# A retention layer with routed adapters: from 128-token steps to 64-token steps with state and v stacked over the partitions, in a fixed order

## The chip, the cores and the metric

The kernel runs on one core of a Trainium2 chip. The metric is the device time of one execution in microseconds (us), and of several executions the median. Engines are named as in the profile: PE is TensorE's matmul and PEld its weight load, DVE is VectorE, ACT is ScalarE, POOL is GpSimd, SP is SyncE, whose queue issues nearly all transfers.

## What is computed

Eight batches of eight heads, 576 tokens, 64 values per head. A causal linear attention with a decay per head, then, for each of the 4608 tokens, a low-rank adapter step over its 512 values: eight adapters of rank 16, of which the two with the highest gate value are used.

```python
scores = q @ k.T / 8                     # per batch and head, 576 x 576
ret = scores * gamma[h] ** (i - j)       # for j <= i, else 0
x = ret @ v                              # heads side by side: 4608 x 512
logits = x @ w_gate                      # 4608 x 8, the best two kept
w = softmax of those two
out = x + sum over the two e of  w[e] * (x @ A[e]) @ B[e]
```

## The kernel before

All arithmetic is f32 but for the last two small products of the adapters, which are fp16. Tokens are cut in chunks of 128: four full chunks and one of 64. A unit is one chunk of two batches (16 heads), so there are 16 units of 128 tokens and then 4 units of 64 tokens, 20 in all, ordered by chunk. Inputs are loaded by quads, two units at a time (L127; the last chunk at L148), with three buffers for each of q, k and v. Each f32 product of two matrices is one call and shows as two records in the profile; a transpose is one.

What is done for a unit:

- scale_v (L197, POOL): v is multiplied by gamma to the power of minus the token's place in the chunk.
- stage_T (L229): PE turns q and k, 16 calls each, into tiles with the head's values on the partitions; DVE takes q out of PSUM and multiplies it by gamma to the power of the token's place (L241), ACT copies k (L250).
- stage_S (L291): the scores, 16 calls with 64 rows of contraction (the values of one head), 128 output rows and 128 columns; DVE masks them, four operations of 128x512 (L302).
- stage_O: where there is a state, its product with q goes into px, 16 calls of 64 rows, 64 output rows, 128 columns (L359). Then the update of the state, k's transpose times v, 16 calls of 128 rows, 64 output rows, 64 columns (L373). DVE adds it to the old state (L387), and POOL decays the sum (L388).
- stage_R (L408): scores times v, on top of px, 16 calls of 128 rows, 64 output rows and 128 columns; ACT copies px to xT (L417).
- stage_Z (L447): x times the adapters' A and the gate, 8 calls of 128x128 with 136 columns; DVE finds the best two and forms the weighted result zc (L460 to L479), with ACT's sigmoid between (L468).
- stage_X (L493, L498): zc turned and copied. stage_B (L512): x turned back to one token per row, 16 calls. stage_Y (L533): the adapters' B added on top; ACT copies the result out (L543), and SP stores it (L548).

In a unit of 64 tokens, the two batches lie in the two halves of the partitions. Its scores are 64x64 tiles with 64 columns (L291 again, 16 calls, row half by head parity and column half by batch, the head parity changing at every call), and so are its state product (L341) and its R (L426).

The order of the main loop is written out as the lines below show, but the instructions are placed by a scheduler that may let stages of neighbouring units mix, and PSUM tiles come from one pool of eight banks:

```python
stage_S(t); scale_v(t + 1); stage_O(t); stage_R(t)
stage_T(t + 1); stage_B(t - 1); stage_X(t - 1)
stage_Z(t); stage_Y(t - 1)
```

The whole kernel before, with the profile's line numbers:

Of the kernel before, what the change touches and what calls it, by code (L numbers as in the profile page):

```python
# [13 lines left out]
AFT = mybir.ActivationFunctionType  # L15


@with_exitstack
def kernel(
# [17 lines left out]
    NP = B // 2  # L37
    NFULL = S // 128
    LH = S - 128 * NFULL
    QUAD = 4  # L40
    NQ = B // QUAD

    scale = 1.0 / float(np.sqrt(Dh))
    gam = 1.0 - 2.0 ** (-5.0 - np.arange(H, dtype=np.float64))
    jj = np.arange(128, dtype=np.float64)

    ident32_np = np.eye(128, dtype=np.float32)
    tri_np = (jj[None, :] >= jj[:, None]).astype(np.float32)
    j64 = np.arange(128) % 64
    i64 = np.arange(64)  # L50
    trih_np = (i64[None, :] >= j64[:, None]).astype(np.float32)
    aqp_np = np.zeros((128, HP, 128), dtype=np.float32)
    g128_np = np.zeros((128, HP), dtype=np.float32)
    for hp in range(HP):
        for ho in range(2):
            g = gam[2 * hp + ho]
            aqp_np[64 * ho : 64 * ho + 64, hp, :] = scale * g ** jj[None, :]
            g128_np[64 * ho : 64 * ho + 64, hp] = g**128.0
    gv_np = np.stack([gam[h] ** (-jj) for h in range(H)], axis=1).astype(np.float32)
    gvh_np = np.stack([gam[h] ** (-j64.astype(np.float64)) for h in range(H)], axis=1).astype(  # L60
        np.float32
    )
    i64_np = np.concatenate([np.eye(64), np.eye(64)], axis=0).astype(np.float32)
    first_np = i64_np
    rest_np = np.concatenate(
        [ident32_np, tri_np, trih_np, gv_np, gvh_np, g128_np], axis=1
    ).astype(np.float32)
    NPK = rest_np.shape[1]
    dr_first = nc.inline_tensor(first_np, "c_first")
    dr_rest = nc.inline_tensor(rest_np, "c_rest")  # L70
    dr_aqp = nc.inline_tensor(aqp_np, "c_aqp")
# [4 lines left out]
    mo = ctx.enter_context(tc.tile_pool(name="moe", bufs=3))  # L76
    pp = ctx.enter_context(tc.tile_pool(name="pp", bufs=8, space=bass.MemoryType.PSUM))

    id64 = cpool.tile([128, 64], FP32, tag="id64", name="id64")
    nc.sync.dma_start(out=id64, in_=dr_first.ap())  # L80
    warm = cpool.tile([128, 1], FP32, tag="warm", name="warm")
    nc.vector.memset(warm, 0.0)
    nc.scalar.activation(out=warm, in_=warm, func=AFT.Sigmoid)
    pack = cpool.tile([128, NPK], FP32, tag="pack", name="pack")
    aqp = cpool.tile([128, HP, 128], FP32, tag="aqp", name="aqp")
    ident32 = pack[:, 0:128]
    tri = pack[:, 128:256]
    trih = pack[:, 256:320]
    gv = pack[:, 320 : 320 + H]
    gvh = pack[:, 320 + H : 320 + 2 * H]  # L90
    g128 = pack[:, 320 + 2 * H : 320 + 2 * H + HP]

    AW = []
    for par in range(2):
        AW.append(cpool.tile([128, HP, ER + E], FP32, tag=f"AW{par}", name=f"AW{par}"))
    Bcat = cpool.tile([128, Dm], FP16, tag="Bcat", name="Bcat")
    ident16 = cpool.tile([128, 128], FP16, tag="ident16", name="ident16")

    def load_moe():
        for dt in range(HP):  # L100
            nc.sync.dma_start(  # L101
                out=AW[0][:, dt, 0:ER].rearrange("p (e r) -> p e r", e=E),
                in_=moe_A[:, 128 * dt : 128 * dt + 128, :].rearrange("e d r -> d e r"),
            )
        nc.sync.dma_start(
            out=AW[0][:, :, ER : ER + E],
            in_=moe_w_gate.rearrange("(t p) e -> p t e", p=128),
        )
        nc.gpsimd.dma_start(out=Bcat, in_=moe_B.rearrange("e r d -> (e r) d"))


    nat = {}

    def issue_full(c, qd, split):
        tiles = []
        for src, tag in ((q, "q32"), (k, "k32"), (v, "v32")):
            tiles.append((src, iop.tile([128, QUAD * H, Dh], FP32, tag=tag, name=tag)))
        parts = ((0, 2), (2, 4)) if split else ((0, 4),)
        for lo, hi in parts:
            for src, tl in tiles:  # L120
                if split and lo == 0 and src is k:
                    nc.sync.dma_start(out=aqp, in_=dr_aqp.ap())
                if split and lo == 0 and src is v:
                    nc.sync.dma_start(out=pack, in_=dr_rest.ap())
                if split and lo == 2 and src is q:
                    load_moe()
                nc.sync.dma_start(  # L127
                    out=tl[:, lo * H : hi * H, :],
                    in_=src[
                        QUAD * qd + lo : QUAD * qd + hi, :, 128 * c : 128 * c + 128, :  # L130
                    ].rearrange("b h j d -> j (b h) d"),
                )
        for half in range(2):
            nat[(c, 2 * qd + half)] = [
                tl[:, half * 2 * H : half * 2 * H + 2 * H, :] for _, tl in tiles
            ]

    def issue_half(qd):

        s0 = 128 * NFULL  # L140
        tiles = []
# [178 lines left out]
    def col(full, b, ho):  # L320
        return (ho ^ b) if full else ho
# [289 lines left out]
```

## Time and profile before

| what | value |
|---|---|
| three runs | 206.46, 207.71, 211.46 us; median 207.71 |
| profiled execution | span 205.06 us from its first to its last instruction (205.1 on the page); no other time of this execution is given |
| granted TensorE clock | 0.995 over the span |
| DVE busy | 108.7 us (53%) |
| ACT busy | 76.6 us (37%) |
| POOL busy | 59.6 us (29%) |
| bytes moved | 39.14 MB, mean 191 GB/s |

A line of the table of groups or of the timeline names the source line, the engine, the operation, what is written and what is read, the shape and the count. On PE, "64*128 64x128" is a tile of 64 contraction rows and 128 output rows with a moving operand of 64 rows and 128 columns. A group's busy time is the time in which at least one of its instructions runs. Records of PE overlap, so that the time that a stage takes from the engine is read from its start to the start of the next stage. In a timeline, the two numbers ahead are start and length, and what stands in brackets is the idle time before and what ended it. In the table of stretches each engine's busy time is followed by its count of instructions.

### The profile page before, as it was taken

To read this page: it belongs to the slowest core of one execution; us is meant where nothing else is said; L and a number is where in the kernel's file an instruction comes from. 1 tells how busy PE (TensorE), PEld (TensorE's weight loads), DVE (VectorE), ACT (ScalarE), POOL (GpSimd) and SP (SyncE) were. 2 spreads that over 40 slices of the span, in tenths; PEclk is the share of its full clock that TensorE was granted. 3 is DMA by queue.
4 is the path that set the end of the run, shared out by engine and by line. 5 is a ranking of instruction groups with operands and counts; after the bars stand their busy time and mean duration, and the time that the engine had idled before them with its cause. 6 is when DMAs were issued, how large, how long until landed. Compare 5 with 4: busy or idle time off the path is not lost.

```text
span 205.1 us, 8039 instructions
## 1 busy us (share of the span) xinstructions
PE 183.8 (90%) x3564; PEld 166.2 (81%) x3564; DVE 108.7 (53%) x286; ACT 76.6 (37%) x206; POOL 59.6 (29%) x60
## 2 busy tenths in 40 slices
PE   0476989799999999999999999999999999999950
PEld 0376969598999999999999999999999899888830
DVE  0226364937374746465656565656565655456630
ACT  2022324153525262625252525253434344454430
POOL 1144323521818202727202720643222402000000
PEclk9999999999999999999999999999999999999997
DMA  5989999799998988991799969756545311222222
GB/s 114 277 109 246 249 243 280 194 290 290 253 319 245 261 249 274 284 297 36 220 286 254 266 215 293 213 145 179 150 118 158 96 51 60 101 79 76 58 47 61
DMA packets 57442, 39.14 MB, mean 191 GB/s; under 512 B 30912, under 2 KB 52672, under 8 KB 57408
## 3 DMA queue, kind: packets, MB, share of 16 engines
q1 hardware_dynamic: 57264, 38.50, 68.0%
q8 instruction: 28, 0.46, 0.9%
q0 software_dynamic: 144, 0.13, 0.4%
q14 instruction: 6, 0.05, 0.1%
HBM read 29.32 MB, written 9.44 MB: 189 GB/s over the span
## 4 chain that ended last, share of the span: by engine, by line
PE 72%; SPq 9%; DVE 7%; DMA 5%; ACT 3%; issue 1%; ACTq 0%
PE pz L447 16%; PE px L408 12%; PE ps_s L291 12%; PE pu L373 6%; PE px L359 6%; PE pt_q L229 5%; DMA k<-in_k_dram 5%; PE po L512 4%; SPq L127 4%; PE pt_k L229 4%; PE po L533 3%; DVE rt L302 2%; PE px L426 2%; ACT osb L543 2%; SPq L101 2%; PE pzt L493 2%
## 5 line engine op out<-in xcount | busy, mean ns | idle before, releaser
L197 POOL TENSOR_TENSOR v<-v,pack 128x512 f32<-128x512 f32 x36 | 36.6, 1042 | 28.0 <-DMA v<-in_v_dram 28.0
L417 ACT COPY xT<-px 128x512 f32<-128x512 f32 x32 | 18.7, 585 | 66.0 <-PE px L408 66.0
L388 POOL TENSOR_TENSOR P<-pn,gdec 128x512 f32<-128x512 f32 x16 | 20.3, 1271 | 75.3 <-DVE pn L387 58.9
L302 DVE TENSOR_TENSOR rt<-ps_s,pack 128x512 f32<-128x512 f32 x64 | 39.7, 682 | 4.2 <-PE ps_s L291 4.2
L291 PE MATMUL ps_s<-qT,kT 64*128 64x128 f32 (+1 forms) x640 | 37.4, 275 | 1.2 <-ACT kT L250 1.2
L447 PE MATMUL pz<-AW,xT 128*128 128x136 f32 x288 | 37.8, 283 | 0.4 <-ACT zT L498 0.4
L291 PEld LDWEIGHTS ps_s<-qT,kT 64*128 64x128 f32 (+1 forms) x640 | 33.7, 184 | 5.3 <-DVE lg L460 3.4
L241 DVE TENSOR_TENSOR qT<-pt_q,aqp 128x512 f32<-128x512 f32 x32 | 20.6, 686 | 31.1 <-PE pt_q L229 31.1
L408 PE MATMUL px<-rt,v 128*64 128x128 f32 x512 | 34.1, 275 | 1.8 <-DVE rt L302 1.7
L447 PEld LDWEIGHTS pz<-AW,xT 128*128 128x128 f32 x288 | 34.7, 190 | 0.6 <-ACT zT L498 0.5
L543 ACT COPY osb<-po 128x256 f32<-128x256 f32 x72 | 23.1, 375 | 25.8 <-PE po L533 25.8
L408 PEld LDWEIGHTS px<-rt,v 128*64 128x64 f32 x512 | 29.0, 137 | 3.8 <-DVE rt L302 2.5
L250 ACT COPY kT<-pt_k 128x512 f32<-128x512 f32 x32 | 17.2, 589 | 19.2 <-PE pt_k L229 19.2
L460 DVE COPY lg<-pz 128x16 f32<-128x16 f32 (+1 forms) x20 | 3.5, 173 | 35.0 <-PE pz L447 35.0
L229 PE MATMUL pt_q<-id,q 64*128 64x64 f32 x288 | 13.6, 234 | 6.7 <-DMA q<-in_q_dram 6.7
L373 PE MATMUL pu<-v,k 128*64 128x64 f32 x512 | 18.9, 225 | 0.0
L373 PEld LDWEIGHTS pu<-v,k 128*64 128x64 f32 x512 | 16.5, 137 | 2.7 <-issue 2.1
L229 PEld LDWEIGHTS pt_q<-id,q 64*128 64x128 f32 x288 | 10.8, 142 | 9.6 <-issue 9.4
L229 PE MATMUL pt_k<-id,k 64*128 64x64 f32 x288 | 12.8, 228 | 3.4 <-DMA k<-in_k_dram 3.4
L473 DVE SCALAR_TENSOR_TENSOR cm<-lg,m,sg 128x8 f32<-128x8 f32 x36 | 9.9, 294 | 8.8 <-ACT sg L468 8.8
L229 PEld LDWEIGHTS pt_k<-id,k 64*128 64x128 f32 x288 | 10.9, 143 | 3.8 <-issue 1.7
L359 PE MATMUL px<-qT,P 64*64 64x128 f32 x384 | 13.2, 275 | 0.0
(34 smaller groups left out, 139.9 us busy)
## 6 DMA issues: line engine op xcount, KB each, us to landing
out_dram<-osb SPq DMA_DIRECT2D x32, 256.0 KB, 3.2
q<-in_q_dram SPq DMA_DIRECT2D x2, 512.0 KB, 5.0
k<-in_k_dram SPq DMA_DIRECT2D x2, 512.0 KB, 6.0
v<-in_v_dram SPq DMA_DIRECT2D x2, 512.0 KB, 5.4
q<-in_q_dram SPq DMA_DIRECT2D x8, 128.0 KB, 3.4
k<-in_k_dram SPq DMA_DIRECT2D x8, 128.0 KB, 3.3
v<-in_v_dram SPq DMA_DIRECT2D x8, 128.0 KB, 4.1
out_dram<-osb SPq DMA_DIRECT2D x8, 128.0 KB, 2.4
```

Of the source, the lines that this page charges most:

```text
L197: nc.gpsimd.tensor_tensor(out=v32[:, b * H : b * H + H, :], in0=v32[:, b * H : b * H + H, :], in1=g.unsqueeze(2).broadcast_to((128, H, Dh) ...
L229: nc.tensor.matmul(ps[r][:, hp, b, :] if full else ps[r][:, hp, :], lhsT=src[sl, b * H + 2 * hp : b * H + 2 * hp + 2, :], rhs=id64[sl, :], ...
L241: nc.vector.tensor_tensor(out=o, in0=ps[r], in1=aqp[:, :, 64 * r : 64 * r + 64] .unsqueeze(2) .broadcast_to((128, HP, 2, 64)), op=ALU.mult,)
L291: nc.tensor.matmul(o, lhsT=kT[sl, hp, b, :], rhs=qT[sl, hp, b, :], start=(a == 0 and (b == 0 or not full)), stop=True, skip_group_check=True,)
L302: nc.vector.tensor_tensor(out=r.rearrange("p a b i -> p (a b) i"), in0=ps[ho].rearrange("p a b i -> p (a b) i"), in1=tri.unsqueeze(1).broa ...
L359: nc.tensor.matmul(px[b][64 * cc : 64 * cc + 64, hp, :], lhsT=P[bp][64 * ho : 64 * ho + 64, hp, b, :], rhs=qT[64 * ho : 64 * ho + 64, hp, ...
L373: nc.tensor.matmul(pu[64 * ho : 64 * ho + 64, hp, b, :], lhsT=s["k"][:, b * H + h, :], rhs=s["v"][:, b * H + h, :], start=(hp == 0 and b = ...
L388: nc.gpsimd.tensor_tensor(out=pf, in0=pn, in1=gdec.rearrange("p a b d -> p (a b d)"), op=ALU.mult,)
L408: nc.tensor.matmul(px[b][64 * cc : 64 * cc + 64, hp, :], lhsT=s["v"][:, b * H + h, :], rhs=rt[h][:, b, :], start=(c == 0 and hp == 0), sto ...
L417: nc.scalar.copy(out=xt, in_=px[b])
L447: nc.tensor.matmul(pz[:, b, :], lhsT=xts[b][:, dt, :], rhs=AW[b][:, dt, :], start=(dt == 0), stop=(dt == HP - 1), skip_group_check=True,)
L543: nc.scalar.copy(out=osb[:, b, :, cc ^ b, :], in_=po[cc][:, b])
```

## The change

The kernel is rewritten around steps of 64 tokens.

- The decays go by the token's absolute place: q is multiplied by gamma to that power over 8 and k by gamma to its negative, both in the layout in which they are loaded, on POOL (L200), two operations of 128x512 each for a unit. v stays as it is, and the state is not decayed. The scaling of v, the factor in q's way out of PSUM, and the decay of the state are gone.
- A unit of 128 tokens has two steps, g = 0 and 1. For each head and step there is a stack W of 128 partitions: the state on one half, the step's 64 rows of v on the other; v is loaded straight into its half, by four transfers in place of one. A stack Q has the turned q on one half and the masked scores on the other. One product of W with Q, 128 rows deep, gives x of the step with the state's part in it (L361): 32 calls of 128 rows, 64 output rows and 64 columns, in place of R and of the state product.
- The scores are 32 calls of 64x64 tiles with 64 columns (L290), the head parity (row half) changing at every call and the batch (column half) at every second. DVE masks them by four operations of 64x512 (L305).
- The state's update is 32 calls of 64x64 with 64 columns, the step (row half) changing at every call and the head parity (column half) at every second (L322). Half of v is first copied by POOL to the partitions where it is needed for that (L218, two operations of 64x512). DVE adds old state and update into the next stack, four operations of 64x512: after step 0 to step 1 of the unit, after step 1 to the next chunk's stack (L344).
- q is copied out of PSUM by ACT, four operations of 64x512 (L258). The output is copied by two operations of 128x512 in place of four of 128x256, and zc is formed by one operation in place of two.
- The last chunk has two units of four batches (two batches in each half of the partitions) in place of four units, so there are 18 units. They have no update of the state.
- The scheduler is off: each engine runs its instructions as they are written. PSUM banks are given by hand: 0 and 1 to the turned q and then the state's update, 2 and 3 to the turned k and then pz and pzt, 4 and 5 to po, 6 and 7 to the scores and then x.
- In round r the work of four units meets: the transposes of r + 2, scores and update of r + 1, x of r, adapters of r - 1, output of r - 2. There are 20 rounds. Loads for quad r/2 + 3 are issued in round r: q at its start and k at its end where r is even, v in the next. W has four buffers, q and k three.
- The first load of q is issued by ACT; the tables shrink to one of 128x208; the adapters' A is used in one copy in place of two.

The core of the diff:

```diff
-    for b in range(nb):                                      # scale_v
-        nc.gpsimd.tensor_tensor(out=v32[...], in0=v32[...], in1=g..., op=ALU.mult)
+    for s in range(2):                                       # scale(t, "q" or "k")
+        eng.tensor_tensor(out=x[:, s], in0=x[:, s], in1=tab[:, c, :]..., op=ALU.mult)
+    for g in range(2):                                       # v_other
+        nc.gpsimd.tensor_copy(out=V2[half(g)], in_=W[t][half(1 - g), g, g])
-    nc.vector.tensor_tensor(out=o, in0=ps[r], in1=aqp[...], op=ALU.mult)   # stage_T, q
+    for ho in range(2):                                      # ev_Tq(t, g)
+        nc.scalar.copy(out=st[t]["Q"][half(ho), g, ho], in_=st[t]["ptq"][g][half(ho)])
-    nc.tensor.matmul(ps[ho][:, a, b, :], lhsT=kT[sl, hp, b, :], rhs=qT[sl, hp, b, :])
+    for g in range(2):                                       # pe_S
+        for hp in range(HP):
+            for s in range(2):
+                for ho in range(2):
+                    nc.tensor.matmul(
+                        ps[ho][half(s), g, hp, :],
+                        lhsT=kT[half(ho), g, s, hp, :],
+                        rhs=Q[half(ho), g, ho, s, hp, :],
...
+    for ho in range(2):                                      # ev_S
+        for s in range(2):
+            nc.vector.tensor_tensor(
+                out=st[t]["Q"][half(1 - ho), :, ho, s, :, :],
+                in0=st[t]["ps"][ho][half(s)], in1=tri[half(s), :]..., op=ALU.mult)
-    nc.tensor.matmul(pu[64 * ho : 64 * ho + 64, hp, b, :], lhsT=s["k"][:, b * H + h, :], rhs=s["v"][:, b * H + h, :])
+    for s in range(2):                                       # pe_U
+        for hp in range(HP):
+            for ho in range(2):
+                for g in range(2):
+                    vs = V2[half(g), s, hp, :] if ho == g else W[t][half(g), g, ho, s, hp, :]
+                    nc.tensor.matmul(pu[g][half(ho), s, hp, :], lhsT=kn[half(g), s, 2 * hp + ho, :], rhs=vs)
-    nc.vector.tensor_tensor(out=pn, in0=puf, in1=pf, op=ALU.add)
-    nc.gpsimd.tensor_tensor(out=pf, in0=pn, in1=gdec..., op=ALU.mult)
+    for ho in range(2):                                      # ev_U(t, g)
+        nc.vector.tensor_tensor(out=f(dst[half(ho), dg, ho]), in0=f(st[t]["pu"][g][half(ho)]),
+                                in1=f(W[t][half(ho), g, ho]), op=ALU.add)
-    nc.tensor.matmul(px[b][...], lhsT=P[bp][...], rhs=qT[...], start=(hp == 0), stop=False)
-    nc.tensor.matmul(px[b][...], lhsT=s["v"][:, b * H + h, :], rhs=rt[h][:, b, :])
+    for s in range(2):                                       # pe_RI
+        for hp in range(HP):
+            for g in range(2):
+                for ho in range(2):
+                    nc.tensor.matmul(px[s][half(ho), hp, g, :],
+                                     lhsT=W[t][:, g, ho, s, hp, :], rhs=Q[:, g, ho, s, hp, :])
...
+    for r in range(NU + 2):
+        if r % 2 == 0: load_qk(r // 2 + 3, "q")
+        else: load_v(r // 2 + 3)
+        v_other(r + 2); scale(r + 3, "k", nc.gpsimd); scale(r + 3, "q", nc.gpsimd)
...
+        pe_T(r + 2, "k"); ev_Tk(r + 2); pe_B(r - 2); pe_T(r + 2, "q")
...
+        pe_S(r + 1); ev_Tq(r + 2, 0); ev_S(r + 1)
+        pe_pzt(r - 2); ev_pzt(r - 2); ev_Tq(r + 2, 1)
+        pe_Z(r - 1, 0); pe_Y(r - 2); pe_Z(r - 1, 1)
+        ev_Y(r - 2); route1(r - 1); route_sig(r - 1)
+        pe_U(r + 1); ev_U(r + 1, 0); route2(r - 1); ev_U(r + 1, 1)
+        pe_RI(r); ev_x(r); store(r - 2)
+        if r % 2 == 0: load_qk(r // 2 + 3, "k")
```

In round 0 the order differs: the first units' scores, update and x come ahead of the transposes. Names that begin with pe_ are PE's work and ev_ the reading of its PSUM banks.

## The prediction

> **What bounds the kernel now.** I read the page's busy shares and slices first, then the table of 20 us stretches, then TensorE's timeline for one unit, then VectorE's for the same unit.
>
> ```profile
> span 205.1 us, 8039 instructions
> PE 183.8 (90%) x3564; PEld 166.2 (81%) x3564; DVE 108.7 (53%) x286; ACT 76.6 (37%) x206; POOL 59.6 (29%) x60
> ...
> DMA  5989999799998988991799969756545311222222
> ```
> ```profile
> 100.00:120.00 20.00, 20.00 (x400) 18.44 (x398) 11.82 (x31) 8.21 (x22) 6.59 (x6) 1.00 0.91 262
> ```
>
> In the stretch 100 to 120 (columns: length, then PE, PEld, DVE, ACT, POOL busy, then the granted clock, the DMA share and GB/s), TensorE is busy 20.00 of 20.00 us at clock 1.00. DVE has 8 us free. So PE's order is the pace, about 10.05 us a unit. The DMA digits say that the first 100 us are nearly full as well; that becomes a rival.
>
> One unit on PE (start, length, records). A stage's price is its start to the next start, since the lengths overlap:
>
> ```profile
> 101.60 0.71 PE L229 MATMUL pt_q<-id,q 64*128 64x64 f32 x16
> 102.15 0.66 PE L229 MATMUL pt_k<-id,k 64*128 64x64 f32 x16
> 102.64 0.66 PE L512 MATMUL po<-id,xT 64*128 64x64 f32 x16
> 103.23 0.29 PE L493 MATMUL pzt<-ident,zc 128*128 128x128 f16 x2
> 103.36 2.07 PE L447 MATMUL pz<-AW,xT 128*128 128x136 f32 x16
> 105.27 0.60 PE L533 MATMUL po<-Bcat,zT 128*128 128x256 f16 x4
> 105.80 2.06 PE L291 MATMUL ps_s<-qT,kT 64*128 64x128 f32 x32
> 107.78 1.10 PE L359 MATMUL px<-qT,P 64*64 64x128 f32 x32
> 108.81 1.15 PE L373 MATMUL pu<-v,k 128*64 128x64 f32 x32
> 109.80 1.92 PE L408 MATMUL px<-rt,v 128*64 128x128 f32 x32
> ```
>
> Transposes of q and k 1.04, po 0.59, pzt 0.13, pz 1.91, po 0.53, scores 1.98, state product 1.03, state update 0.99, R 1.85: 10.05. Each f32 product shows as two records (16 calls, x32).
>
> The last chunk's units have 64 tokens, and their stages are the nearest rows to the new shapes:
>
> ```profile
> 186.69 0.69 PE L291 MATMUL ps_s<-qT,kT 64*64 64x64 f32 x32
> 187.20 1.11 PE L341 MATMUL pq<-qT,P 64*64 64x64 f32 x32
> 188.50 1.12 PE L426 MATMUL px<-rh,v 64*64 64x64 f32 x32 [0.19 <-DVE rh L310]
> ```
>
> L291 with 64x64 tiles takes 0.51 us for 32 records, 16 ns each. L341 and L426 have the same shape and take about 33 ns (L426: 188.50 to the next start at 189.55). Their orders differ: L291 changes the row half at every call and the column half at every second; L341 uses only the two diagonal quarters; L426 stays on a row half for two calls.
>
> VectorE in the same unit:
>
> ```profile
> 105.47 0.17 DVE L460 COPY lg<-pz 128x16 f32<-128x16 f32 x1 [1.83 <-PE pz L447]
> 105.68 0.24 DVE L462 MAX8 m<-lg 128x8 f32<-128x8 f32 x2
> 105.95 0.16 DVE L463 SCALAR_TENSOR_TENSOR ns<-m 128x2 f32<-128x2 f32 x1
> 106.56 0.41 DVE L473 SCALAR_TENSOR_TENSOR cm<-lg,m,sg 128x8 f32<-128x8 f32 x2 [0.45 <-ACT sg L468]
> 106.89 0.48 DVE L479 TENSOR_TENSOR zc<-pz,cm 128x128 f16<-128x128 f32 x2
> 107.29 2.48 DVE L302 TENSOR_TENSOR rt<-ps_s,pack 128x512 f32<-128x512 f32 x4
> ```
>
> **The change, PE's work.** Transposes, po, pzt, pz and the adapter's output keep their calls: 4.20 us. Scores: 64 records of 64x64 with 64 columns, in L291's order (row half innermost, column half next): 64 x 16 ns = 1.02 (was 1.98). State update: 32 calls of 64x64 instead of 16 of 128x64, again row half innermost: 1.02 by the same row (was 0.99). The bounds of both are 16 and 33 ns; I take 16, the row with the same alternation. x: 32 calls of 128 rows, 64 output rows, 64 columns: the shape of today's L373, 0.99 us for 32 records, so 1.98 for 64 (state product and R were 2.88). Sum 8.22, against 10.05. The gap of 1.8 us over 14 rounds would be 26 us.
>
> **What VectorE adds.** It loses the q scaling (two of 0.69), which moves to POOL, and has in exchange four masks of 64x512 (a shorter partition range at the same 512 columns: 2.48 us, L302's row) and four state additions of 64x512 instead of one of 128x512 (1.29 a pair, as two 128x512 with PSUM input take at L241). Routing stays, about 0.64 to ns and 0.81 for cm and zc. DVE then has 2.48 + 2.58 + 1.45 = 6.5 us a round.
>
> **Where these meet.** The order is now fixed, and banks 0 and 1 hold first the transposed q, then the state update. In a round PE issues k's transposes, po, q's transposes, scores, pzt, pz, po, pz, state update, x. The q transposes of the next round need both additions out of banks 0 and 1; behind them in PE's queue stand the scores, and DVE's masks wait for those. That is a ring. From the start of the scores: scores 1.02, 0.2 to DVE (pz's last issue before 105.27, lg at 105.47), masks 2.48, ends 3.70. PE meanwhile does pzt, both pz and po: 1.02 + 0.13 + 1.91 + 0.53 = 3.59, so lg starts 3.79, ns ends 4.43. State update on PE 3.59 to 4.61, DVE at 4.81: additions of step 0 to 6.10, cm and zc to 6.91, additions of step 1 to 8.20. Then 0.06 to PE, q's transposes 0.52: the next scores start at 8.8. PE alone would be back at 8.22, so it waits 0.6 us at the q transposes. The k transposes wait for zc (bank 2), at 6.9 against 6.57, inside that. Round: 8.8 us.
>
> **ACT.** Copies of x 1.17 (two of 585 ns), k 1.07, q now four of 64x512 at half a microsecond each 2.1, zT 0.39, output two of 128x512 1.1, sigmoid 0.5: 6.3 us a round, in an order where each is ready before PE asks. Hidden; without cover the nearest is the second q copy, done 2.8 us after the scores' start, where the state update needs it at 3.59.
>
> **POOL.** v's scaling and the state decay go; k and q are scaled there (four of 1042 ns) and two halves of v copied (two of about 635): 5.4 us a round, free-running behind the loads. Hidden after the start, not at it.
>
> **Loads and SP.** The queue now issues q, k, four v quarters and four stores per two rounds, with the same bytes. By the trace's packets, 1 MB loads cost 3.86 us of all 16 engines, loads of 16 pieces per row 4.74 per MB and stores 3.0: 3.86 + 3.86 + 4.74 + 3.0 = 15.5 us per two rounds of 17.6. Stores now wait for ACT with a k load behind them on SP; the buffers (three, four for v) leave two rounds before anyone misses it. I count nothing.
>
> **Start.** Before, v of the second quad landed at 34.3 (POOL's wait at L197). The new order carries 0.3 MB less of tables but 256-byte pieces for v: about 33.5. POOL has v's copy ahead of unit 3's scaling: 33.5 + 1.3 + 2.08 + 2.08 = 38.9, then half of the q transposes: unit 2's scores at 39.2 (34.2 before, but unit 4's at 55.6 there, and 39.2 + 17.6 = 56.8 here: level).
>
> **End.** Unit 16's scores start at 39.2 + 14 x 8.8 = 162.4. The round after has no state update: unit 17's follow 6.35 later (1.02 + 0.13 + 2.44 + 1.98 + 0.2 + 0.58 for x's copy), at 168.8. From there PE's list runs to 13.95, then unit 17's routing, transpose and output: 0.2 + 0.64 + 0.5 + 0.81 + 0.3 + 0.39 + 0.75 + 1.07 = 4.6, at 187.3. The trace has 4.9 us from the last copy (199.53 + 0.65) to the end of the span: 192.2. The median of the three runs, 207.71, lies 2.65 above the profiled span of 205.06; no other time of that execution is given, so I add 2.65: 195.
>
> [...]
>
> **Rivals.** (1) Forecast: the ring at about 8.8, 195 us; chance 0.44 (190 to 201). (2) VectorE is not in the way, because half-partition operations are quicker or overlap more: PE's 8.22 paces it, 195 - 14 x 0.6 = 187; 0.13. No row with 64 partitions on DVE speaks for it. (3) VectorE's ring is longer: single operations at 690 ns rather than 620 to 645 back to back, and waits of 0.2 where I took 0.06, give about 9.4, 203; 0.18. (4) DMA paces: if the queue sustains only 0.8 of its engines, two rounds take 15.5 / 0.8 = 19.4, 9.7 each, 208; against it, stretches at 0.91 and slices at 9; 0.10. (5) Slower: the quarter-array products run at 33 ns as at L426, not 16. Scores and update are both in the ring: + 2 x 1.05, 10.9 a round, 195 + 14 x 2.1 = 224. It decides (over 2% slower, 211.9) from 1.2 us a round, 25 ns a record; one of the two alone gives 210. For it: two of three rows of this shape. Against: the alternation. 0.15 in all, a third of it the one alone. That the change does not cut PE's records is no case: they rise from 198 to 262 a unit; only the price of each falls.
>
> **Numbers.** 2% of 207.71 is about what a measurement of this kernel can tell from no change: below 203.5 faster, above 211.9 slower. Faster: 0.44 + 0.13 + 0.07 of case 3 = 0.64. Same: the rest of case 3 (0.11), half of 4, one product alone: 0.21. Slower: 0.15. The range of 8 in 10 runs from case 2 to one product alone: 186 to 212; the forecast's own is 190 to 201.
>
> **What would show it.** The new profile should have scores of 64 records in about 1.0 us, x in about 2.0, PE waiting some 0.6 us at the q transposes for the state addition, rounds of 8.8, DVE near 6.5 busy in each, and unit 2's scores near 39. Starts of 64x64 records 33 ns apart, PE waiting for DMA or POOL after 60 us, or no wait at the q transposes would each make a step wrong.

## The result, and the profile after

The changed kernel takes 243.38 us (median of four runs, 239.16 to 247.83) against 208.03 for the kernel before (206.46 to 211.46). The ratio is 1.156, with an interval of 1.144 to 1.167: slower, where 195 us and faster had been forecast. Medians here are of all executions; ratios and their intervals leave out the slow ones, those over 1.5% above the fastest of their kernel. The profiled execution is the slowest of the four (247.83, span 246.1).

From the page of the kernel after, busy shares, slices of TensorE's granted clock and of the transfer engines:

```profile
span 246.1 us, 10238 instructions
PE 178.8 (73%) x4588; PEld 163.2 (66%) x4588; DVE 130.2 (53%) x269; ACT 116.4 (47%) x236; POOL 92.8 (38%) x110
...
PEclk9999995599999979959989799979889999999996
DMA  8997999999999998889769668948633751212334
```

TensorE is busy for less time than before (178.8 us against 183.8) and now stands idle for 67 us. The clock has dips, and the transfer engines, which move nearly the same bytes (38.91 MB against 39.14), are full for longer.

The kernel after, the same stretch of 20 us as was shown of before, and one earlier one:

```profile
40.00:60.00 20.00, 15.80 (x367) 14.31 (x368) 8.30 (x18) 8.53 (x17) 12.86 (x15) 0.74 1.16 198
...
100.00:120.00 20.00, 14.01 (x355) 12.98 (x347) 11.82 (x22) 8.64 (x17) 10.49 (x12) 0.83 0.93 210
```

PE was busy all of 20.00 us with 400 records; it is busy 14.01 with 355, and a unit has 262 records now, not 198. No engine is full. The transfers are: a share of 0.93 to 1.16 for 198 to 210 GB/s, where before 0.91 gave 262. (The share adds up the packets' times, so it can pass 1.)

One round late in the kernel after, where nothing disturbs it (state update left out: its 64 records appear as many rows between 201.1 and 202.2):

```profile
197.42 1.16 PE L290 MATMUL ps_s<-Q,kT 64*64 64x64 f32 x64
198.51 0.28 PE L388 MATMUL pzt<-ident,zc 128*128 128x128 f16 x2
198.64 1.15 PE L407 MATMUL pz<-AW,xT 128*128 128x136 f32 x8
199.62 0.60 PE L468 MATMUL po<-Bp,zT 128*128 128x256 f16 x4
200.06 1.09 PE L407 MATMUL pz<-AW,xT 128*128 128x136 f32 x8
...
202.17 2.08 PE L361 MATMUL px<-Q,W 128*64 128x64 f32 x64
204.90 0.71 PE L234 MATMUL pt_k<-pack,k 64*128 64x64 f32 x16 [0.64 <-DVE zc L454]
205.42 0.69 PE L269 MATMUL po<-pack,xT 64*128 64x64 f32 x16
205.92 0.80 PE L234 MATMUL pt_q<-pack,q 64*128 64x64 f32 x16
206.65 1.16 PE L290 MATMUL ps_s<-Q,kT 64*64 64x64 f32 x64
```

Scores 1.09 from start to start (forecast 1.02), x 2.09 to its end (1.98), the transposes of k 0.52 and those into po 0.50. Only q's transposes take longer, 0.73 (0.52). So the prices of TensorE's new products are as forecast: 64 records of the quarter array in 1.09 us, 17 ns each. This round lasts 9.23 (forecast 8.8). Most others last 10 to 15.

The kernel after, what PE waited for, the longest sums:

```profile
PE pt_k L234 <- DVE zc L454: 11.6, 12, 1.3
PE pt_k L234 <- DVE k L200: 9.4, 1, 9.4
PE pu L322 <- issue: 6.6, 5, 2.5
PE pt_k L234 <- POOL k L200: 5.8, 2, 5.5
PE po L269 <- issue: 4.4, 2, 2.3
```

Two things stand here that the forecast did not have: a wait for zc at k's transposes, about 1 us in each of 12 rounds, and idle time that ends with no releaser ("issue"), 23.3 us over all lines. The waits for k (DVE, POOL) are the start. None of PE's waits ends with a transfer.

### The profile page after: what moved, and what is told of

It reads as the page before. It is cut to its first block, busy times and chain, and to the rows that moved or that the text cites. A ratio compares the mean times of both kernels' runs of the same rounds, so it can differ in the third digit from the quotient of the medians.

```text
span 246.1 us, 10238 instructions
## 1 busy us (share of the span) xinstructions
PE 178.8 (73%) x4588; PEld 163.2 (66%) x4588; DVE 130.2 (53%) x269; ACT 116.4 (47%) x236; POOL 92.8 (38%) x110
## 2 busy tenths in 40 slices
DMA packets 78970, 38.91 MB, mean 158 GB/s; under 512 B 59728, under 2 KB 74320, under 8 KB 78928
## 3 DMA queue, kind: packets, MB, share of 16 engines
q1 hardware_dynamic: 76720, 37.62, 76.5%
## 4 chain that ended last, share of the span: by engine, by line
PE 53%; DVE 15%; SPq 13%; issue 11%; DMA 3%; POOL 2%; ACT 1%; ACTq 0%; POOLq 0%
PE pz L407 15%; PE ps_s L290 9%; DVE W L344 7%; PE pu L322 7%; PE px L361 5%; DVE cm L450 4%; PE pt_q L234 4%; PE pt_k L234 4%; SPq L175 4%; PE po L269 4%; SPq L133 3%; SPq L170 3%; PE po L468 3%; DMA W<-in_v_dram 3%; DVE zc L454 2%
## 5 line engine op out<-in xcount | busy, mean ns | idle before, releaser
L305 DVE TENSOR_TENSOR Q<-ps_s,pack 64x512 f32<-64x512 f32 x72 | 49.6, 689 | 72.6 <-PE ps_s L290 71.6
L218 POOL COPY V<-W 64x512 f32<-64x512 f32 x32 | 20.0, 624 | 82.9 <-PE pu L322 38.9
L344 DVE TENSOR_TENSOR W<-pu,W 64x512 f32<-64x512 f32 x64 | 43.9, 687 | 12.4 <-PE pu L322 11.8
L258 ACT COPY Q<-pt_q 64x512 f32<-64x512 f32 x72 | 41.7, 579 | 16.8 <-PE pt_q L234 15.5
L361 PE MATMUL px<-Q,W 128*64 128x64 f32 x1152 | 39.9, 229 | 3.7 <-issue 3.7
L200 POOL TENSOR_TENSOR k<-k,pack 128x512 f32<-128x512 f32 x34 | 35.0, 1049 | 16.3 <-DMA k<-in_k_dram 15.3
L361 PEld LDWEIGHTS px<-Q,W 128*64 128x64 f32 x1152 | 37.1, 143 | 5.5 <-issue 4.0
L200 POOL TENSOR_TENSOR q<-q,pack 128x512 f32<-128x512 f32 x36 | 36.7, 1040 | 9.4 <-DMA q<-in_q_dram 9.4
L290 PE MATMUL ps_s<-Q,kT 64*64 64x64 f32 x1152 | 29.0, 257 | 5.3 <-issue 3.5
L290 PEld LDWEIGHTS ps_s<-Q,kT 64*64 64x64 f32 x1152 | 25.0, 166 | 9.9 <-ACT Q L258 4.7
L322 PE MATMUL pu<-V,k 64*64 64x64 f32 x512 | 21.8, 233 | 5.0 <-issue 5.0
L322 PEld LDWEIGHTS pu<-V,k 64*64 64x64 f32 x512 | 18.9, 145 | 7.9 <-issue 6.0
L322 PE MATMUL pu<-W,k 64*64 64x64 f32 x512 | 21.1, 233 | 1.6 <-issue 1.6
```

What stands on the lines that cost most here:

```text
L200: eng.tensor_tensor(out=x[:, s], in0=x[:, s], in1=tab[:, c, :].unsqueeze(2).broadcast_to((128, H, Dh)), op=ALU.mult,)
L218: nc.gpsimd.tensor_copy(out=V2[half(g)].rearrange("p s a d -> p (s a d)"), in_=W[t][half(1 - g), g, g].rearrange("p s a d -> p (s a d)"),)
L258: nc.scalar.copy(out=st[t]["Q"][half(ho), g, ho], in_=st[t]["ptq"][g][half(ho)])
L290: nc.tensor.matmul(ps[ho][half(s), g, hp, :], lhsT=kT[half(ho), g, s, hp, :], rhs=Q[half(ho), g, ho, s, hp, :], start=True, stop=True, ski ...
L305: nc.vector.tensor_tensor(out=st[t]["Q"][half(1 - ho), :, ho, s, :, :], in0=st[t]["ps"][ho][half(s)], in1=tri[half(s), :].unsqueeze(1).uns ...
L322: nc.tensor.matmul(pu[g][half(ho), s, hp, :], lhsT=kn[half(g), s, 2 * hp + ho, :], rhs=vs, start=True, stop=True, skip_group_check=True,)
```

## The experiments

A time without a ratio is of one execution; the others are medians, with the ratio to the kernel before on the same chip. What is read from a profile (gaps, rounds, packets) is of one execution too. "Gaps" is PE's idle time without a releaser.

### First theory: v's four small transfers. It fell.

Theory T was that v in four transfers to 64 partitions each makes the loads late. Three kernels tried it from both sides.

a_vreuse, the changed kernel with v's loads left out from the fifth quad on:

```diff
+            if n >= 4:
+                tl = load_v.tiles[n - 4]      # an old tile is read again
+            else:
+                tl = iop.tile(..., bufs=4)
...
+        if n >= 4: return
```

> The changed kernel with v's loads of the fifth and every later quad left out (the stacks of four quads earlier are used again, so the output is of other v). T, the transfers: v's quarter loads run at half the rate that was reckoned (four issues in 9.5 us for 1 MB), the queue falls behind, and q and k come late; then the rounds from the sixth on fall to 9.2 to 10 us, the gaps of 2 to 3 us marked issue on PE mostly go, and the span is about 210. F, the instruction stream: PE starves for its own instructions because it has 29% more records per unit; then a gap stays in nearly every round and the span stays above 230. R, the ring of DVE and PE is simply longer: rounds near 12 us also without v's loads.

229.45 us, gaps 10.8. Late rounds last 9.97 while POOL scales and 9.13 to 9.38 when it has nothing left to do. So fewer bytes help, and even without waits for loads the round isn't 8.8.

a_vnat, the changed kernel with v loaded whole like q and k, all four quarters copied into the stacks by POOL:

```diff
-        for g in range(2):
-            for ho in range(2): eng.dma_start(out=tl[half(1 - ho), g, ho]..., in_=v[b0:b1, ho::2, j0 : j0 + 64, :]...)
+        eng.dma_start(out=vt[:, ...], in_=v[b0 + 2 * lo : b0 + 2 * hi, :, 128 * c : 128 * c + 128, :]...)
+            for ho in range(2):                          # v_other, POOL
+                nc.gpsimd.tensor_copy(out=W[t][half(1 - ho), g, ho], in_=vn[half(g), ho])
```

> The changed kernel with v loaded as q and k are, in one transfer of 128 partitions a quad, and POOL copying all of it into the stacks (four operations of 64x512 a unit in place of two). T: the load of v issues in 3.5 to 5 us per MB in place of 9.5, two rounds need about 15 us of the queue, the time is 205 to 218. F: PE's stream is the same, so the gaps stay and the time is above 235. R: rounds of 12, above 235.

234.47 us, ratio 1.132 (1.123 to 1.140), gaps 15.2. Unit 2's scores still start near 46 us. Nine us less, most of the loss remains.

b_vquarter, the kernel before with v, but for the first quad, loaded by four transfers to 64 partitions, as the change does:

```diff
+                    for g in range(2):
+                        for ho in range(2):
+                            nc.sync.dma_start(out=tv[64 * g : 64 * g + 64, ho]...,
+                                in_=v[QUAD * qd : QUAD * qd + QUAD, ho::2, j0 : j0 + 64, :]...)
```

> The kernel before with v of each full quad but the first loaded by four transfers of 64 partitions and 16 pieces, as the changed kernel does. T: the four issues take about 9.5 us per MB here too; the queue then needs 3.9 + 3.9 + 9.5 + 3 = 20.3 us per two units, as long as PE takes for them, and the time rises by 3 to 15 us. F and R: no change, 208.

205.47 us, ratio 0.987 (0.982 to 0.991): no loss at all. The row of this kernel that answers to the one shown of before:

```profile
100.00:120.00 20.00, 20.00 (x400) 18.43 (x398) 11.44 (x31) 8.18 (x22) 6.54 (x6) 1.00 0.80 224
```

PE is as full as before. b_vparity, the same in two transfers of 128 partitions (`for ho in range(2)` alone, 256-byte pieces):

> The kernel before with v of each full quad but the first loaded by two transfers of all 128 partitions, each with every second head (16 pieces of 256 bytes a row). If T holds because of the small packets, as slow per MB as the quarters; if because a transfer fills only half of the partitions, 4.7 us per MB as the first quad's loads of 16 pieces show, and a time of 208 to 211.

208.72 us, ratio 1.005 (1.001 to 1.010). So neither the small pieces nor the half-filled partitions cost the kernel before anything. T fell.

### Record count alone

b_split, the kernel before with scores and R cut in halves of 64 columns, so that a unit has 262 records as after the change:

```diff
-                for b in range(2):
+                for b, i in [(b, i) for b in range(2) for i in range(2 if full else 1)]:
-                            rhs=qT[sl, hp, b, :],
+                            rhs=qT[sl, hp, b, 64 * i : 64 * i + 64],
```

> The kernel before with the scores and R of the 128-token units cut into halves of 64 columns: the same arithmetic, but 262 records a unit on PE in place of 198, as many as the changed kernel has. By the rows, PE's time for them grows by 0.1 to 0.3 us a unit (64 columns cost about half of 128). F, the instruction stream: PE runs out of instructions here as well, gaps marked issue of 0.5 to 2.5 us at several of the fetches, a lower granted clock behind them, and 5 to 40 us more. If record count alone does no harm: 208 to 213, no such gaps.

233.06 us, ratio 1.126 (1.121 to 1.131), but gaps of only 0.2 us. Two rows of this kernel, scores and the next start:

```profile
108.37 3.79 PE L292 MATMUL ps_s<-qT,kT 64*128 64x64 f32 x64
112.09 1.10 PE L360 MATMUL px<-qT,P 64*64 64x128 f32 x32
```

The cut scores take 3.72 us, 58 ns a record: tiles of 64x128 got no cheaper with half the columns (1.98 for 32 whole ones). The unit became longer, 11.4 us (459 records in the 20 us from 100), so the stream is hardly denser than before. This says nothing on what 262 records in 9 us do, except that their number alone makes no gaps at 11.4.

### What the loads and the scaling cost

a_noload, the changed kernel with the loads of q, k and v left out from the fourth quad on (`if n >= 3:` reuse the tile of three quads before, as in a_vreuse); a_noload_noscale, in which POOL also leaves out the scaling from the seventh unit on (`if t >= NU or t >= 6: return`):

> The changed kernel with every load of q, k and v from the fourth quad on left out (the tiles of three quads earlier are used again and scaled again, so the output is of other data). F as far as it is the fetch of instructions held up by the data transfers: fetches of about 0.9 us as before in quiet stretches, hardly a gap on PE, the clock near full, rounds of 9.1 (POOL idle) to 10.0 us (POOL scaling), span about 205. If the gaps have nothing to do with the transfers: still 10 or more of 1 to 2 us and a span above 220.

> As the run without loads, and POOL's scaling of q and k left out from the seventh unit on as well. If POOL's scaling holds up DVE's small operations between two scalings (cm 1.16 us for two where 0.36 is seen without POOL): cm back at 0.4 in every round, every round near 9.1, the span 8 to 11 us below the run without loads alone. If not: no change.

217.05 us with rounds of 9.97, all but a few, and gaps of 1.0; 208.41 with rounds of 9.17. The loads cost 26 us and nearly all the gaps; the scaling costs 0.8 us in every round, though behind the start none of PE's waits ends with POOL. VectorE's cm and zc in a_noload, then its masks to zc in a_noload_noscale:

```profile
143.17 1.16 DVE L460 SCALAR_TENSOR_TENSOR cm<-lg,m,sg 128x8 f32<-128x8 f32 x2
144.36 0.42 DVE L464 TENSOR_TENSOR zc<-pz,cm 128x256 f16<-128x256 f32 x1
```

```profile
112.52 2.82 DVE L315 TENSOR_TENSOR Q<-ps_s,pack 64x512 f32<-64x512 f32 x4 [1.97 <-PE ps_s L300]
...
116.18 1.39 DVE L354 TENSOR_TENSOR W<-pu,W 64x512 f32<-64x512 f32 x2 [0.17 <-PE pu L332]
117.60 0.37 DVE L460 SCALAR_TENSOR_TENSOR cm<-lg,m,sg 128x8 f32<-128x8 f32 x2
118.00 0.42 DVE L464 TENSOR_TENSOR zc<-pz,cm 128x256 f16<-128x256 f32 x1
```

Two operations on 128x8 take 1.16 us beside POOL and 0.37 alone. The kernel after shows the same within itself, first VectorE, then POOL:

```profile
193.75 1.16 DVE L450 SCALAR_TENSOR_TENSOR cm<-lg,m,sg 128x8 f32<-128x8 f32 x2
...
203.81 0.36 DVE L450 SCALAR_TENSOR_TENSOR cm<-lg,m,sg 128x8 f32<-128x8 f32 x2
```

```profile
193.80 2.08 POOL L200 TENSOR_TENSOR k<-k,pack 128x512 f32<-128x512 f32 x2
...
201.42 2.04 POOL L200 TENSOR_TENSOR q<-q,pack 128x512 f32<-128x512 f32 x2
```

At 193.80 POOL's scaling starts 0.05 us behind cm, and cm ends with the first of POOL's two operations (194.90 and 194.88); at 203.81 the scaling has ended (201.42 + 2.04 = 203.46). cm is of the few DVE operations whose inputs both lie in SBUF: the masks and the additions, with one input in PSUM, are not lengthened (2.81 and 1.39 in both kernels). Of the 36 cm operations of the kernel after, 20 overlap one of POOL, and ten of these take 0.37 to 1.02 us; the other 26 take 0.21 to 0.23. Its 72 masks take 0.68 to 0.70, 18 of them beside POOL. By what POOL holds cm up, and why in ten of the 20 only, is not shown.

### Another order. It failed.

a_vnat_order put k's transposes behind the scores and both adapter products behind the state update, on the base of a_vnat:

```diff
-        pe_T(r + 2, "k"); pe_B(r - 2); pe_T(r + 2, "q"); pe_S(r + 1); pe_pzt(r - 2); pe_Z(r - 1, 0)
-        pe_Y(r - 2); pe_Z(r - 1, 1); pe_U(r + 1); pe_RI(r)
+        pe_T(r + 2, "q"); pe_B(r - 2); pe_pzt(r - 2); pe_S(r + 1); pe_T(r + 2, "k")
+        pe_Y(r - 2); pe_U(r + 1); pe_Z(r - 1, 0); pe_Z(r - 1, 1); pe_RI(r)
```

> The kernel with v loaded whole and copied by POOL, in another fixed order: scores ahead of k's transposes, the transposes of q first in the round, the update of the state ahead of pz, both state additions on DVE ahead of the routing, so that PE waits for no DVE operation of the same round. R, the ring: rounds without a gap fall from 9.1 to 10.0 to about 8.5, the time by 8 to 18 us from 234. F: the gaps marked issue stay, so the time stays above 208.

246.35 us, ratio 1.190 (1.182 to 1.199). The order made a new wait, from the waits of this kernel:

```profile
PE pzt L382 <- DVE zc L448: 18.3, 18, 1.6
```

Routing now came last in VectorE's round, and zc was 1 us late in each of 18.

### Second theory: where the load tiles lie

In every variant of the changed kernel, and in none of before's, the packets of the loads were long. By the trace's packet records (mean ns of one packet):

| kernel | 1024 bytes | 256 bytes |
|---|---|---|
| before, b_vquarter, b_vparity, b_split | 58.6 to 59.2 | 18.0 to 18.4 |
| after, a_vreuse, a_vnat, a_noload | 76.5 to 80.6 | 24.4 to 27.1 |

It is not v's shape, for q's and k's packets are long too (78.2 ns for 1024 bytes in the kernel after, where v's have 256). What the first family shares is the place of its tiles. They are allocated behind the constants, which take 19584 bytes of each partition before and 4320 after, an estimate from the two kernels' own shapes with each tile rounded up to a multiple of 32. The difference is 59 x 256 + 160. All load tiles are multiples of 8192 bytes. So if they start at a multiple of 256 before the change, all start 96 bytes past one after it. That they start at a multiple before, the rounding, and 256 as the measure are the author's assumptions; no trace shows an address. Places below are meant by this layout. Theory A says that the 96 bytes make the packets long. Three kernels:

```diff
     warm = cpool.tile([128, 1], FP32, tag="warm", name="warm")      # a_pad: after, aligned
+    cpool.tile([128, 40], FP32, tag="pad", name="pad")              # 160 bytes; a_pad32: 8 columns
```

```diff
+    cpool.tile([128, 24], FP32, tag="pad", name="pad")              # b_pad: before, 96 bytes behind the constants
```

> The changed kernel with 160 unused bytes per partition behind the last constant, so that the tiles that the loads write (k, q, W) start at a multiple of 256 bytes in the partition; in the changed kernel they start 96 bytes past one, in the kernel before at a multiple. Nothing else is changed. Theory A (the place of the tiles makes the packets long): 1024-byte packets take 46 to 54 ns instead of 76 to 81, 256-byte packets 18 instead of 25 to 33; unit 2's scores start near 40 us instead of 46; TensorE's idle time without a releaser falls from 23 us to under 10; time 210 to 228 (217 was measured without the loads of the later quads, and it had the late start). Rival B (packets are long because the engines use the memory at the same time, or because of the order of the loads): packets as before at 76 to 81 and 25 to 33 ns, time 239 to 248.

> The kernel before with 96 unused bytes per partition behind the last constant, so that its load tiles start 96 bytes past a multiple of 256, as in the changed kernel. Theory A: 1024-byte packets 76 to 81 ns instead of 46 to 54, 256-byte ones 25 or more instead of 18; the stretches up to 100 us, which are nearly full of transfers, become longer, unit 2's scores start 4 to 6 us later, time 212 to 228. Rival B: packets and time as before, 206 to 209.

a_pad: 220.27 us, ratio 1.063 (1.054 to 1.071); packets 58.5 and 18.2 ns; unit 2's scores at 40.7 instead of 46.2; gaps 7.4 instead of 23.3 (the profiles are of a_pad's fastest execution, 217.34, and of the slowest of the kernel after, 247.83). b_pad: 214.85 us, ratio 1.027 (1.016 to 1.037), packets of 1024 bytes 76.3, unit 2's scores at 39.5 instead of 34.2. Theory A held in both kernels, but for one part: b_pad's 256-byte packets stayed at 19.0. The unused bytes move the work tiles too, but DVE's masks take 688 ns each in a_pad and 689 in after. Rows of a_pad, then of the kernel before and of b_pad:

```profile
40.00:60.00 20.00, 18.26 (x526) 16.99 (x526) 13.91 (x30) 11.46 (x23) 13.25 (x16) 0.93 0.86 225
```

```profile
40.00:60.00 20.00, 19.67 (x363) 17.86 (x364) 11.65 (x32) 8.18 (x22) 6.54 (x6) 1.00 0.98 282
```

```profile
40.00:60.00 20.00, 18.77 (x327) 16.66 (x324) 12.31 (x27) 7.71 (x21) 9.10 (x10) 1.00 0.98 219
```

In a_pad a share of 0.86 moves 225 GB/s, where after needed 1.16 for 198. In b_pad the share of 0.98, which in the kernel before moved 282, moves 219. By the medians, 160 unused bytes are worth 23 us of the 35 that the change lost; by the ratios (1.156 and 1.063), some 19 of 32.

By the means of the kernels before and after, a packet of 256 bytes takes 26.2 / 18.1 = 1.45 times as long at the moved place, one of 1024 bytes 78.2 / 59.2 = 1.32 times. Why it takes longer is not shown.

> a_pad with 32 unused bytes instead of 160: the load tiles start at a multiple of 128, but 128 past one of 256. [...] If a multiple of 64 or 128 is enough, 18 and 54 ns, and 216 to 222 as a_pad.

230.62 us, packets of 1024 bytes 75.3 ns (54 expected) and of 256 bytes 23.1 (18 expected). A multiple of 64 or 128 was not enough: the time lies between a_pad's 220.27 and the 243.38 of the kernel after, the 1024-byte packets are nearly as long as at 96 bytes past a multiple (78.2), and of the 256-byte packets about half take 18 or 19 ns and the others longer. What decides it from packet to packet stays open.

### The ring, with aligned tiles

a_pad_swap moves the scores ahead of q's transposes and cm and zc ahead of the state additions; a_pad_best also moves the second adapter product ahead of the adapter's output:

```diff
-        pe_T(r + 2, "q"); pe_S(r + 1)
+        pe_S(r + 1); pe_T(r + 2, "q")
-        ev_U(r + 1, 0); route2(r - 1); ev_U(r + 1, 1)
+        route2(r - 1); ev_U(r + 1, 0); ev_U(r + 1, 1)
-        pe_Z(r - 1, 0); pe_Y(r - 2); pe_Z(r - 1, 1)                  # a_pad_best
+        pe_Z(r - 1, 0); pe_Z(r - 1, 1); pe_Y(r - 2)                  # a_pad_best
```

> The aligned changed kernel (a_pad) with two moves in its fixed order: the scores are issued ahead of q's transposes, and the second half of routing (cm, zc) ahead of both state additions. Ring theory: TensorE no longer waits for the state additions at q's transposes nor for zc at k's, and rounds without gaps go from 9.2 to 10 us to 8.3 to 8.7, TensorE's own sum; the slower cm beside GpSimd then lies beside TensorE's work. If the gaps of the instruction stream go with the alignment, 188 to 198; if they stay, 205 to 225. If the ring theory is wrong (masks are still the limit), rounds stay at 9 or more and the time is within 2% of a_pad.

> a_pad_swap with one more move: the second adapter product of a round is issued ahead of the adapter's output (L469) instead of behind it, so that the copy of zT, for which TensorE waited 0.45 us in 14 rounds, lies beside it. Ring theory: rounds without gaps fall from 9.17 us to 8.7, TensorE's own sum of measured starts (scores 1.09, q 0.65, pzt 0.12, pz 2.1, po 0.45, update 1.1, x 2.0, k 0.55, po 0.5, and some tenths), so 14 x 0.45 = 6 us less than a_pad_swap: 203 to 206. If another wait takes its place (ScalarE's copies of q, done just when the state update needs their banks, or the masks on VectorE), rounds stay above 9 and the time is 209 to 213.

a_pad_swap: 210.82 us, ratio 1.008 (1.000 to 1.016), gaps 4.7. The waits for zc and for the additions are gone, one takes their place, from this kernel's waits:

```profile
PE po L469 <- ACT zT L399: 6.3, 14, 0.5
```

So the best rounds are 9.17 again, now for another reason, but POOL no longer lengthens them. The time falls by 9.5 us. a_pad_best removes that wait too, and its best round is 8.75; yet it takes 213.03 us, ratio 1.011 (1.001 to 1.022), and its gaps are 15.7 in place of 4.7. (The two profiled executions took 213.39 and 208.37 us; others of a_pad_best went down to 208.55 and others of a_pad_swap up to 215.87, so the size of that rise is not sure.) The expected 6 us did not come; the gaps took them. That made the gaps the question, and two kernels tested them: a_best_noload (a_pad_best without loads from the fourth quad on, the edit of a_noload) and a_vnat_best (a_pad_best with v as in a_vnat).

> a_pad_best with the loads of q, k and v from the fourth quad on left out (the tiles of three quads before are read again, so most output rows are those of other tokens); the instructions of all computing engines are those of a_pad_best. If the gaps come from loads that meet a dense stream of records, the 16 us of gaps fall below 2, rounds are 8.7 (8.6 to 8.9) throughout, and the time is 192 to 198, the predicted time reached with the predicted mechanism. If the dense stream alone makes the gaps, 8 us of them or more stay and the time is over 203.

> a_pad_best with v loaded as in a_vnat: one transfer of 1024-byte packets per quad instead of four of 256-byte packets, GpSimd copies all four quarters into the stacks (two more copies of 0.62 us a unit). By the packets, 1 MB of v costs 3.5 us of 16 engines instead of 4.7. If the share of the transfer engines sets the gaps, they fall from 16 us to under 10 and the time to 203 to 208; GpSimd then works 6.6 us of a round of 8.7 and its scaling must not be late. If gaps do not depend on that share, 210 to 214.

a_best_noload: 196.94 us, gaps 1.4. The row for the stretch in a_pad_best, then in a_best_noload, and the two ends of one of its rounds:

```profile
100.00:120.00 20.00, 16.04 (x443) 14.75 (x441) 14.37 (x30) 11.52 (x24) 11.11 (x14) 1.00 0.83 241
```

```profile
100.00:120.00 20.00, 20.00 (x613) 18.61 (x611) 16.62 (x35) 14.43 (x30) 12.95 (x15) 1.00 0.21 78
```

```profile
102.08 1.16 PE L301 MATMUL ps_s<-Q,kT 64*64 64x64 f32 x64
103.17 0.71 PE L245 MATMUL pt_q<-pack,q 64*128 64x64 f32 x16
...
107.69 2.08 PE L372 MATMUL px<-Q,W 128*64 128x64 f32 x64
109.70 0.76 PE L245 MATMUL pt_k<-pack,k 64*128 64x64 f32 x16
110.25 0.72 PE L280 MATMUL po<-pack,xT 64*128 64x64 f32 x16
110.90 0.29 PE L301 MATMUL ps_s<-Q,kT 64*64 64x64 f32 x4
```

PE is full at 613 records in 20 us, and rounds are 8.75 to 8.84 from 58 us to 137 us. The same instructions with the loads take 16 us more (213.03). So the gaps need loads in flight. That they need a dense stream too, the kernel before and b_split say, which have no gap to speak of beside loads at 400 and 459 records in 20 us. a_vnat_best: gaps 9.0, as expected, but 213.44 us, ratio 1.030 (1.022 to 1.038). Its fewer gaps were paid for elsewhere (POOL is busy 116.3 us instead of 92.3, its shortest rounds are 8.9 to 9.6), so on time it is a miss.

What a gap looks like in the kernel after:

```profile
132.53 0.56 PE L234 MATMUL pt_k<-pack,k 64*128 64x64 f32 x11 [1.30 <-DVE zc L454]
135.32 0.34 PE L234 MATMUL pt_k<-pack,k 64*128 64x64 f32 x5 [2.24 <-issue]
...
137.19 1.98 PE L290 MATMUL ps_s<-Q,kT 64*64 64x64 f32 x64
```

After eleven of sixteen equal calls PE stops, with all their inputs there, and goes on 2.24 us later. The page of the kernel after counts 36 packets of 16384 bytes in a queue of kind "instruction" (28 in the kernel before):

```profile
q8 instruction: 36, 0.59, 1.2%
```

36 x 16384 bytes is 64 bytes for each of the 2 x 4588 records of PE and PEld (within 1%), and 28 x 16384 is 64 for each of the 2 x 3564 before, so this is PE's own instruction stream, 256 records to a packet. One of these packets ran from 132.42 to 133.89, and PE resumed 1.43 us after its end. The other long gaps end in the same way: packet ends at 98.09, 119.54, 157.41 and 175.51, PE resumes at 99.39, 120.92, 158.75 and 176.88. A packet takes 1.27 us on the mean in the kernel after and 1.06 in the one before. The third row shows the second price: the granted clock has fallen to 0.50 (mean from 136 to 138 us), and the scores take 1.98 us instead of 1.16.

Counted through the traces, the place is always the same. The changed kernel and its eleven variants have 79 stops of more than 0.4 us without a releaser, and each comes at the 194th or 195th of a stretch of 256 records (PE's and PEld's together, with the semaphore records of their queue, from the first on); PE goes on 1.2 to 1.7 us after the end of a packet. Between 45 and 155 us, the packet for the next 256 records starts 0.85 us (median; at most 2.6) after PE has passed that place in a_best_noload, 2.2 (at most 4.1) in a_pad_best and 3.2 (at most 4.8) in after. So loads make the packet start late. In a_best_noload 256 records last 4.2 us, in the kernel before 6.4. An estimate from these rows: with 1.1 us for the packet and 1.25 behind it, the first leaves room for a start 1.9 us late, the second for one 4.1 us late. By this estimate that is why the dense stream stops beside loads and the one before does not.

## Why the prediction was wrong

It was wrong in sign, by 48 us. Point by point:

- **"Transposes, po, pzt, pz ... keep their calls", scores, update and x at 16 to 17 ns a record: right.** Scores 1.09, x 2.0 to 2.1, with the alternation taken from the row at 186.69. The rival in which the quarter-array products run at 33 ns, the only one on the slow side, did not happen: 64 records in 1.09 us are 17 ns each.
- **"Loads and SP ... with the same bytes. I count nothing": the step that failed.** Packets were priced by durations from before, as if the tiles' place were a constant. The change moved it to 96 bytes past a multiple of 256, by the layout worked out above, and the means rose from 59.2 to 78.2 ns for 1024 bytes and from 18.1 to 26.2 for 256. a_pad against after: 23 us by the medians (19 by the ratios), of which about 5.5 are the start.
- **"Start: unit 2's scores at 39.2": wrong mostly for that reason.** 46.2 in after, 40.7 with aligned tiles, 37 to 40 in the later aligned kernels.
- **"POOL ... Hidden after the start": failed.** None of PE's waits behind the start ends with POOL, but cm beside it takes 1.16 us and lies in the ring. In a_pad it does so in ten rounds, 0.8 us each, about 8; a_noload_noscale is 8.6 us shorter than a_noload.
- **The ring: right in kind, short by 0.37.** Undisturbed it is 9.17: masks take 2.81 where 2.48 was taken, a pair of additions 1.39 where 1.29 was. Each mask takes as long as before (689 ns on the mean, 682 before), but the four overlap less; why is not shown. Over 14 rounds 5 us. The rival with 9.4 had that mechanism.
- **No step for the instruction stream.** A third to a half more records per us (526 to 613 in 20 us, 400 before) beside busy transfer engines make PE stop for its instructions: 7.4 us in a_pad, 23.3 in after, where the clock falls as well. "DMA paces" was a rival, but through the data, not through this.

The sum closes for the profiled execution of a_pad: 195 + 1.5 (start) + 5 (ring) + 8 (POOL) + 7.4 (gaps) = 216.9, and it took 217.34. From there to after it is the place of the tiles. Between the two profiled executions, 30 us apart, 5.5 are the start and 16 are gaps; the other 9 fit the lower granted clock (0.914 on the mean, 0.955 in a_pad), at which the same 4588 records keep PE busy for 178.8 us instead of 165.7. In the other direction, a_best_noload's 196.94 comes close to the forecast, with nine rounds in a row of 8.75 to 8.84, but these are set by PE's own sum (q's transposes 0.65, not 0.52, and some tenths elsewhere over the 8.22 forecast), not by the ring that the forecast had.

Three things stay open: what makes one packet past a multiple of 256 long and another short; by what POOL holds cm up; and how the loads hold up the stream's packets. That these queue behind the data of the loads fits their late starts, but no run changed the stream's transfers by themselves. No version here beats the kernel before by 2%; the nearest is a_pad_swap, level with it, and b_vquarter, 1.3% faster than it.

## What to carry to other kernels

When a change alters constants or tiles that are allocated ahead of the load buffers, work out by how many bytes the load buffers move, and try unused bytes that take them back: 160 of them took this kernel's 1024-byte packets from 78.2 to 58.5 ns and some 20 us off its time, and 96 ahead of its predecessor's buffers took those packets from 59.2 to 76.3 ns and cost it 6 us. An engine that nobody waits for can still slow a small operation on the critical path: two cm operations, with their inputs in SBUF, took 1.16 us beside GpSimd's scaling and 0.37 alone, so look for such operations beside GpSimd. And a plan that fills TensorE with more and shorter records has to leave room for their instructions to arrive beside the loads: cutting the best round from 9.17 to 8.75 gave nothing while loads ran (gaps 15.7 us in place of 4.7).

## What was not expected of the hardware

- Packets of 256 bytes took 18 ns on the mean in the kernel before and in a_pad, 26 in the kernel after and 19 in b_pad, whose tiles, by the layout worked out above, start 96 bytes past a multiple of 256; packets of 1024 bytes took 59 and 58.5, 78 and 76.
- TensorE stopped for up to 3.0 us in the kernel after where its instruction stream was refilled, always at the same place of a stretch of 256 records, nearly only while loads ran (gaps 23.3 us, in a_noload 1.0), and resumed 1.2 to 1.7 us after the end of a 16384-byte packet. During or shortly behind six of that kernel's seven stops of over 2 us the granted clock fell to half for 3.4 or 6.8 us, and the same 64 records took 1.98 us instead of 1.16; behind a stop of 2.4 us in a_pad it did not fall.
- f32 products with tiles of 64x128 and 64 columns took 58 ns a record in b_split, hardly less than with 128 columns in the kernel before (1.98 us for 32, 62 each), while the scores' 64x64 tiles went at 17 in the kernel after (1.09 us for 64).
